# Retention, then two feed-forward layers on one core: the opening laid out by a list scheduler, the first tile in two parts, state sums of 64x64 per head

## The chip, the cores and the metric

One core of one Trainium2 chip runs the whole kernel. The metric is the device time of one execution in microseconds (us). Its engines work beside each other, each in its own order: TensorE (PE, its weight loads apart as PEld), VectorE (DVE), ScalarE (ACT), GpSimd (POOL), and SyncE (SP), which issues the DMAs. Before: 897.27 us, the median of three runs (895.79 to 897.95). About 0.3% of that, 2.7 us, is what such a measurement can tell from no change.

## The reference

```
scores = q @ k.T / sqrt(64)                  # 4 batches, 8 heads, 576 positions, 64 wide
ret    = scores * gamma_h ** (i - j)         # for i >= j, else 0;  gamma_h = 1 - 2**(-5-h)
x      = (ret @ v), heads side by side       # 2304 tokens x 512
h      = x @ w_in                            # 512 x 2048
x      = (h * cos(h)) @ w_out                # 2048 x 512
xn     = x / sqrt(mean(x*x) + 1e-6) * rms_g
out    = (silu(xn @ w_gate) * (xn @ w_val)) @ w_out2     # hidden width 1536
```

## The kernel before

**Attention.** Each batch has 576 positions: four full chunks of 128 and a rest of 64, twenty chunks in all. Chunk n costs PE four groups of float32 matmuls. `scores(n)` (L256) multiplies keys by queries, two heads at a time in the two row halves of the array; DVE then masks the result (L259). `values(n)` adds the chunk's k'v to a running sum in PSUM, the `total` (L272, one 128x128 product per pair of heads, of which only the two 64x64 blocks on the diagonal are used); ACT copies these into `state` (L282). Then `state` times the queries (L277, not in the first chunk of a batch) and the masked scores times the values (L287, in the two column halves) are summed in one bank, and DVE multiplies that with the decay and writes it to `xall` (L290). POOL scales the values first (L251). The rest chunk has no L272.

**First layer.** Tokens go in five tiles, `TILES`, four of 512 and one of 256; `ORDER_A` is 0, 1, 2, 4, 3. A tile takes 16 units, one for each 128 columns of the hidden width. A unit has `hidden` (12 matmuls: 4 slices of the contraction, each as three float32r products of high and low parts, L192 to L194), then `gate` (h cos h, three steps on ACT and three on DVE in turn, down to a high part `ghi` and a low part `glo`), and three units later (`LAG`) `out_t`, again 12 matmuls, into four accumulators `acc`. Tiles of x are split into high and low parts by `split_x` (ACT L186, DVE L129).

**Weights.** The 16 blocks of `w1` come as 64-bit floats and are turned into two float32r parts by `Block.convert`: ACT L137, DVE L141 and L142, ACT L146, DVE L147 and L148, ACT L164, DVE L129. A tile of 512 tokens can't get past a block that isn't converted. From the second tile on, the 36 pieces of the second layer's weights are converted beside the units (`piece_steps`; the units in which a piece begins stand in `begins`) and stored to DRAM, and `norm` prepares tiles 0 and 1.

**Order.** `PLAN` is the order of the loads on SP: chunk numbers, and -1 for a block of weights. The first batch's five chunks come ahead of the first unit (loop at L311), then each of the next eight units takes two chunks (`ATT_STEPS`, L731 to L763). Up to L784, the compiler's own scheduler orders all engines; after that ACT, DVE and POOL are kept in the written order (`manual_schedule(engines=ENGINES)`) and PE is still ordered by the compiler until the second layer. The chunk tiles and blocks share 14 slots (`wa`); the matmuls of attention and `hidden` share three PSUM banks (`g`) until attention ends.

**Second layer.** It runs three groups of tokens (L1012), PE in the written order, and is not touched.

Of the kernel before, what the change touches and what calls it, by code (L numbers as in the profile page):

```python
# [22 lines left out]
F32 = mybir.dt.float32  # L23
# [42 lines left out]
ATT_STEPS = 8  # L66
CONV_LEAD = 2
WARM = 10
AHEAD = 4
LAG = 3  # L70
LAST_BEGINS = [48, 51, 54, 65, 66, 67]
MANUAL = NF1

PLAN = [0, 1, 2, 3, -1, 4, 5, -1, 6, 7, -1, 8, -1, 9, 10, -1, -1, 11, 12, -1, 13, 14, -1, -1, 15, 16, -1, 17, 18, -1, 19]
# [6 lines left out]
def body(ctx: ExitStack, tc, qkv, qkr, vr, w1, w2, rg, gq, gk, mask, out):  # L81
# [57 lines left out]
    def value2(t):  # L139
        size = t.bitcast(F32)  # L140
        nc.vector.tensor_scalar(size, size, LEAST, LARGEST, op0=ALU.max, op1=ALU.min)  # L141
        nc.vector.tensor_scalar(t, t, 3, 0x3FFFFFF8, op0=ALU.logical_shift_left, op1=ALU.bitwise_and)  # L142

    def value3(t, words):
        low, high = words[..., 0], words[..., 1]
        nc.scalar.activation(low, low.bitcast(U32), AF.Copy, scale=2.0 ** -29)  # L146
        nc.vector.scalar_tensor_tensor(t, high, -2 ** 30, t, op0=ALU.bitwise_and, op1=ALU.bitwise_or)  # L147
        nc.vector.tensor_tensor(t, t, low, op=ALU.add)  # L148

    class Block:  # L150
# [7 lines left out]
        def convert(self, t):  # L158
            value1(t, self.raw)
            value2(t)  # L160
            value3(t, self.raw)
            self.w = self.where.tile([P, 2, 2, 512], F32R, tag="w", name="w")
            z = t.bitcast(F32)
            nc.scalar.copy(self.w[:, :, 0], z)  # L164
            minus(nc.vector, self.w[:, :, 1], self.w[:, :, 0], z)
# [13 lines left out]

    def split_x(t, kcs=range(KC)):  # L180
        t0, n = TILES[t]
        for kc in kcs:
            hi = xsp.tile([P, 512], F32R, tag="xs", name="xhi")
            lo = hi[:, n:] if 2 * n <= 512 else xsp.tile([P, 512], F32R, tag="xs", name="xlo")
            src = xall[:, kc, t0:t0 + n]
            nc.scalar.copy(hi[:, :n], src)  # L186
            minus(nc.vector, lo[:, :n], hi[:, :n], src)
            xs[t, kc] = (hi, lo)
# [25 lines left out]
    gam = [gam0]  # L214
# [4 lines left out]
    state = ap1.tile([P, NPAIR, P], F32, name="state")  # L219
    nc.vector.memset(state, 0.0)  # L220
    nc.vector.memset(half_pi, HALF_PI)
# [4 lines left out]
    def load(n):  # L226
# [14 lines left out]
        if 0 < n < NCH:  # L241
            gam.append(ap1.tile([P, NPAIR, width(c)], F32, name=f"gam{c}"))
            for p in range(NPAIR):
                nc.scalar.activation(gam[c][:, p, :], gam0[:, p, :width(c)], AF.Copy, scale=later[:, c, p:p + 1])

    def scores(n):
        b, c = chunks[n]
        w = width(c)
        kt, qt, vv, _ = ld[n]
        v3 = vv[:w].rearrange("p (h d) -> p h d", h=H)  # L250
        nc.gpsimd.tensor_tensor(v3, v3, vg_sb[:w, c, :].unsqueeze(2).to_broadcast([w, H, D]), op=ALU.mult)  # L251
        ps = [ps_tile().rearrange("p (h i) -> p h i", h=NPAIR) for _ in range(2)]
# [4 lines left out]
        for hh in range(2):  # L257
            s = ap.tile([P, NPAIR, P], F32, tag=f"s{hh}", bufs=2, name=f"s{hh}")
            nc.vector.tensor_tensor(s[:w, :, :w], ps[hh][:w, :, :w],  # L259
                                    mask_sb[:w, :w].unsqueeze(1).to_broadcast([w, NPAIR, w]), op=ALU.mult)  # L260
            sc[n, hh] = s

    def values(n):
        b, c = chunks[n]
        w = width(c)
        _, qt, vv, kk = ld.pop(n)
        if c < NFULL:
            if c == 0:
                total[0] = psa.tile([P, NPAIR, P], F32, tag="st", name="total")
            for p in range(NPAIR):  # L270
                cs = slice(p * P, (p + 1) * P)
                nc.tensor.matmul(total[0][:, p, :], kk[:, cs], vv[:, cs], start=c == 0 and p == 0, stop=True,  # L272
                                 skip_group_check=True)
        po = ps_tile().rearrange("p (a i) -> p a i", a=NPAIR)
        if c > 0:
            for p in range(NPAIR):
                nc.tensor.matmul(po[:, p, :w], state[:, p, :], qt[:, p, :], start=p == 0, stop=False,  # L277
                                 skip_group_check=True)
        if c < NFULL:
            for hh in range(2):  # L280
                r = slice(hh * D, (hh + 1) * D)
                nc.scalar.copy(state[r, :, r], total[0][r, :, r])  # L282
# [6 lines left out]
        t0 = b * S + c * P  # L289
        nc.vector.tensor_tensor(xall[:, :, t0:t0 + w], po[:, :, :w], gam[c], op=ALU.mult)  # L290
        del sc[n, 0], sc[n, 1]

# [5 lines left out]
    plan = list(PLAN)  # L298

    def fetch_chunks(until):  # L300

        while plan and until not in ld:
            n = plan.pop(0)
            if n < 0:
                blocks1.append(Block(w1[len(blocks1)], wa))
            else:
                load(n)

    fetch_chunks(1)
    scores(0)  # L310
    for n in range(PRO):  # L311
        fetch_chunks(n + AHEAD)
        scores(n + 1)
        values(n)
        if n == 3:
            split_x(ORDER_A[0])
            blocks1[0].convert(temps())
    blocks1[1].convert(temps())
    nc.sync.dma_start(rg_sb, rg)
    nc.scalar.mul(rg_sb, rg_sb, 0.375)  # L320

# [100 lines left out]
    pending = []  # L422

    def gate(t, f, ps, beside, copies, between=None, apart=False):

        def step():
            next(beside)
            if copies:
                copies.pop(0)()

        def finish():
            mult, cast, low = pending.pop()
            mult()
            step()
            return cast, low

        if ps is not None:
            n = TILES[t][1]
            r = ch.tile([P, 512], F32, tag="t", name="r")
            k, r = r.bitcast(I32)[:, :n], r[:, :n]  # L440
            parts = {}

            def cast():
                parts["hi"] = ch.tile([P, 512], F32R, tag="hi", bufs=LAG, name="ghi")[:, :n]
                nc.scalar.copy(parts["hi"], r)  # L445

            def low():
                parts["lo"] = ch.tile([P, 512], F32R, tag="lo", bufs=LAG, name="glo")[:, :n]
                minus(nc.vector, parts["lo"], parts["hi"], r)
                g_parts[t, f] = parts["hi"], parts["lo"]  # L450

            nc.scalar.activation(k, ps, AF.Identity, bias=quarter, scale=INV_2PI)
            old = finish() if pending else None
            nc.vector.scalar_tensor_tensor(r, k, -TWO_PI, ps, op0=ALU.mult, op1=ALU.add)  # L454
            step()
            if old:
                old[0]()
                step()
            nc.scalar.activation(r, r, AF.Sin, bias=half_pi, scale=1.0)  # L459
            step()  # L460
            if old:
                old[1]()
                step()
            pending.append((lambda: nc.vector.tensor_tensor(r, ps, r, op=ALU.mult), cast, low))  # L464
            if between:
                between()
        if pending and (ps is None or not apart):
            cast, low = finish()
            cast()
            step()  # L470
            low()
            step()
        for _ in beside:
            pass
        while copies:
            copies.pop(0)()
# [12 lines left out]
    def piece_first(k):  # L489
# [5 lines left out]
        def low():  # L495
            words = loaded[k]
            nc.scalar.activation(words[..., 0], words[..., 0].bitcast(U32), AF.Copy, scale=2.0 ** -29)

        return [size, low]

    def piece_steps(k):
# [4 lines left out]
        value2(t)  # L506
# [6 lines left out]
        nc.vector.scalar_tensor_tensor(t, words[..., 1], -2 ** 30, t, op0=ALU.bitwise_and, op1=ALU.bitwise_or)  # L513
        yield
        nc.vector.tensor_tensor(t, t, words[..., 0], op=ALU.add)
# [8 lines left out]
    begins = [i for i in range(NF1, 3 * NF1) if (i + 1) % NF1]  # L524
    begins += LAST_BEGINS

    def begun(i):
        return begins.index(i) if i in begins else None
# [169 lines left out]
    def out_t(t, f):  # L698

        n = TILES[t][1]  # L700
        if f == 0:
            accs[t] = [acc_tile(m) for m in range(KC)]
        whi, wlo = part1("out", f)
        g = g_parts.pop((t, f))
        for m in range(KC):
            c = slice(m * P, (m + 1) * P)
            mm3(accs[t][m][:, :n], (whi[:, c], wlo[:, c]), g, f == 0, f == NF1 - 1)
        if f == NF1 - 1:
# [396 lines left out]
```

## Time and profile before

| | us |
|---|---|
| median of three runs | 897.27 |
| the profiled execution | 898.45 |
| its span in the trace | 896.7 |
| PE busy | 881.8 |
| DVE busy | 663.5 |
| ACT busy | 472.6 |

The profile shows one execution. Busy time of PE overstates its work, since matmuls are pipelined and their ends modelled: from the start of one matmul to the start of the next is the better measure, and the prediction uses it. A row of the timeline merges instructions of one kind that follow each other: start, duration, engine, line, what it writes and reads, and how many. In brackets stands how long the engine idled before it, and what ended that.

### The profile page before, as it was taken

The page shows a single profiled execution, that of the slowest core. Times are in us where ns is not written, and L with a number is a line of the kernel's source. Part 1 is how long each engine was busy: PE and PEld are TensorE (multiplying, and loading weights), DVE is VectorE, ACT ScalarE, POOL GpSimd, SP SyncE. Part 2 cuts the span into 40 slices and gives each one's busy share as a digit, 9 for nine tenths or more (in the row PEclk, how much of TensorE's full clock was granted, in tenths as well). Part 3 has the DMA queues.
Part 4 walks back from the last instruction along what each step waited for, and adds up shares of the span by engine and source line. Part 5 has one row for each costly group of instructions (what it writes and reads, how often), then busy time and mean ns, then how long its engine had stood idle before and what let it go on. Part 6 is the DMA issues. An engine that isn't in the chain of part 4 may idle for free.

```text
span 896.7 us, 14175 instructions
## 1 busy us (share of the span) xinstructions
PE 881.8 (98%) x5482; PEld 803.3 (90%) x5482; DVE 663.5 (74%) x1001; ACT 472.6 (53%) x819; POOL 94.4 (11%) x97
## 2 busy tenths in 40 slices
PE   7999999999999999999999999999999999999998
PEld 6778888888888888998888999999999999999998
DVE  3999989677789777856785789789565588443584
ACT  4666567565566665655565755544443444333341
POOL 2341100000000000000445435200000000000000
PEclk9999999999999999999999999999999999999999
DMA  8966452044534443202688689998767698777693
GB/s 320 393 249 235 159 217 90 1 141 145 143 115 147 146 149 109 72 1 83 220 263 292 233 296 316 339 320 292 258 246 249 220 298 279 261 250 256 213 300 116
DMA packets 59027, 188.98 MB, mean 211 GB/s; under 512 B 5328, under 2 KB 23376, under 8 KB 50384
## 3 DMA queue, kind: packets, MB, share of 16 engines
q1 hardware_dynamic: 58960, 188.08, 61.9%
q8 instruction: 43, 0.70, 0.3%
q14 instruction: 24, 0.20, 0.1%
HBM read 140.87 MB, written 47.19 MB: 210 GB/s over the span
## 4 chain that ended last, share of the span: by engine, by line
PE 80%; DVE 12%; DMA 3%; ACT 2%; issue 1%; SPq 1%; POOL 1%; DVEq 0%; ACTq 0%; POOLq 0%
PE h L858 14%; PE acc L858 13%; PE acc L903 13%; PE acc L193 9%; PE acc L194 9%; PE acc L192 9%; DVE w L129 3%; PE h L193 3%; PE h L194 3%; PE h L192 3%; PE h L903 2%; DMA raw<-w_dram 2%; DVE s L259 1%; DVE t L147 1%; DMA so<-w 1%
## 5 line engine op out<-in xcount | busy, mean ns | idle before, releaser
L858 PE MATMUL h<-w 128*128 128x384 f32 x720 | 139.5, 335 | 1.1 <-DVE SV L840 1.1
L858 PE MATMUL acc<-w 128*128 128x384 f32 x720 | 139.9, 335 | 0.3
L858 PEld LDWEIGHTS h<-w 128*128 128x128 f32 x720 | 125.7, 188 | 2.6 <-DVE SV L840 2.2
L858 PEld LDWEIGHTS acc<-w 128*128 128x128 f32 x720 | 125.6, 188 | 1.9 <-DVE v L846 1.9
L193 PE MATMUL acc<-glo,w 128*128 128x512 f32 (+1 forms) x320 | 118.2, 369 | 0.8 <-DVE glo L129 0.8
L192 PE MATMUL acc<-ghi,w 128*128 128x512 f32 (+1 forms) x320 | 118.3, 370 | 0.0
L194 PE MATMUL acc<-ghi,w 128*128 128x512 f32 (+1 forms) x320 | 117.9, 368 | 0.0
L577 POOL TENSOR_TENSOR z<-z 128x256 f32<-128x256 f32 x72 | 66.4, 925 | 394.3 <-DMA z<-w 332.0
L903 PE MATMUL acc<-w 128*128 128x256 f32 x846 | 104.2, 283 | 0.0
L903 PEld LDWEIGHTS acc<-w 128*128 128x128 f32 x846 | 103.1, 192 | 0.3 <-DVE w L129 0.2
L193 PEld LDWEIGHTS acc<-glo,w 128*128 128x128 f32 x320 | 60.4, 189 | 11.1 <-DVE glo L129 1.2
L192 PEld LDWEIGHTS acc<-ghi,w 128*128 128x128 f32 x320 | 60.3, 189 | 10.1
L194 PEld LDWEIGHTS acc<-ghi,w 128*128 128x128 f32 x320 | 60.3, 189 | 9.9
L846 DVE TENSOR_TENSOR v<-s,acc 128x384 f32<-128x384 f32 x54 | 29.8, 552 | 52.9 <-PE acc L858 39.0
L459 ACT ACTIVATE r<-r,half_pi 128x512 f32<-128x512 f32 (+1 forms) x80 | 54.9, 686 | 11.4 <-DVE r L454 11.1
L129 DVE TENSOR_TENSOR w<-SV,w 128x768 fp32r<-128x768 f32 x55 | 50.7, 966 | 13.5 <-ACT w L886 13.5
L886 ACT CAST w<-SV 128x768 fp32r<-128x768 f32 x55 | 42.5, 831 | 34.1 <-DVE SV L891 18.3
L824 ACT COPY s<-h 128x384 f32<-128x384 f32 x54 | 25.9, 479 | 58.2 <-PE h L858 56.8
L129 DVE TENSOR_TENSOR glo<-r,ghi 128x512 fp32r<-128x512 f32 (+1 forms) x80 | 52.5, 656 | 3.9 <-ACT ghi L445 2.9
L445 ACT CAST ghi<-r 128x512 fp32r<-128x512 f32 (+1 forms) x80 | 46.3, 578 | 15.5 <-DVE r L464 15.4
L840 DVE TENSOR_TENSOR SV<-s,h 128x384 f32<-128x384 f32 x54 | 29.8, 551 | 31.5 <-PE h L858 26.2
L192 PE MATMUL acc<-xhi,w 128*128 128x512 f32 (+1 forms) x144 | 52.7, 366 | 0.0
(129 smaller groups left out, 1660.5 us busy)
## 6 DMA issues: line engine op xcount, KB each, us to landing
w<-so SPq DMA_DIRECT2D x42, 768.0 KB, 6.2
w<-s SPq DMA_DIRECT2D x24, 1024.0 KB, 5.0
raw<-w_dram SPq DMA_DIRECT2D x36, 512.0 KB, 4.0
w<-s SPq DMA_DIRECT2D x24, 768.0 KB, 4.3
raw<-w_dram SPq DMA_DIRECT2D x16, 1024.0 KB, 6.2
x<-qkv_dram SPq DMA_DIRECT2D x15, 1024.0 KB, 10.5
s<-w SPq DMA_DIRECT2D x12, 1024.0 KB, 6.9
w<-t SPq DMA_DIRECT2D x36, 256.0 KB, 2.3
```

Of the source, the lines that this page charges most:

```text
L129: eng.tensor_tensor(dst, src, hi.bitcast(F32), op=ALU.subtract)
L192: nc.tensor.matmul(dst, a[0], b[0], start=start, stop=False)
L193: nc.tensor.matmul(dst, a[0], b[1], start=False, stop=False)
L194: nc.tensor.matmul(dst, a[1], b[0], start=False, stop=stop)
L445: nc.scalar.copy(parts["hi"], r)
L459: nc.scalar.activation(r, r, AF.Sin, bias=half_pi, scale=1.0)
L577: nc.gpsimd.tensor_tensor(z[:, dst], z[:, a], z[:, b], op=op)
L840: nc.vector.tensor_tensor(dst, s, bank, op=ALU.add)
L846: nc.vector.tensor_tensor(t, s, bank, op=ALU.add)
L858: nc.tensor.matmul(bank, w[:, wp, kc * P:(kc + 1) * P], x[:, kc], start=k in (0, 1, 3) and kc == 0 and m == 0, stop=kc == 1 and m == 2, sk ...
L886: nc.scalar.copy(t[:, 0], src)
L903: nc.tensor.matmul(bank, s[:, a, i % 2, m * P:(m + 1) * P], wi[:, b], start=start and i == 0 and p == 0 and m % 2 == 0, stop=i == NPR - 1 ...
```

## The change

The constants: the first tile is cut into units 0 to 5 and 6 to 15, with all of tile 1 between them; the list of loads and the units in which pieces of the second layer's weights begin follow from that.

```
+FIRST = 6
+SEGMENTS = [(0, 0, FIRST), (1, 0, NF1), (0, FIRST, NF1), (2, 0, NF1), (4, 0, NF1), (3, 0, NF1)]
+STEPS = [(s, t, f) for s, (t, a, b) in enumerate(SEGMENTS) for f in range(a, b)]
+ENDS = [k for k in range(len(STEPS)) if k + 1 == len(STEPS) or STEPS[k][0] != STEPS[k + 1][0]]
+MANUAL = FIRST + NF1
+BEGINS = [k for k in range(MANUAL, 3 * NF1) if k not in ENDS] + list(range(3 * NF1, 4 * NF1, 2)) + list(range(4 * NF1, 4 * NF1 + 4))
-PLAN = [0, 1, 2, 3, -1, 4, 5, -1, 6, 7, -1, 8, -1, 9, 10, -1, -1, 11, 12, -1, 13, 14, -1, -1, 15, 16, -1, 17, 18, -1, 19]
+PLAN = [0, 1, 2, 3, 4, 5, 6, 7, 8, 9, 10, -1, 11, -1, 12, 13, -1, 14, -1, 15, -1, 16, -1, 17, -1, -1, 18, -1, 19, -1, -1, -1, -1, -1, -1, -1]
```

So eight of the 36 pieces begin in the units of tile 4, where three did. The parts of x of tile 0 are stored to DRAM and read back for its second part, and that part is added to what the first left in `xall`:

```
+    def keep_x(t):
+        for kc in range(KC):
+            for part in range(2):
+                nc.sync.dma_start(kept_x[:, kc, part], xs[t, kc][part].bitcast(F32))
+    def fetch_x(t):
+        for kc in range(KC):
+            xs[t, kc] = tuple(xsp.tile([P, 512], F32R, tag="xs", name=name) for name in ("xhi", "xlo"))
+            for part in range(2):
+                nc.sync.dma_start(xs[t, kc][part].bitcast(F32), kept_x[:, kc, part])
...
-            copies = [lambda m=m: nc.scalar.copy(xall[:, m, t0:t0 + n], accs[t][m][:, :n]) for m in range(KC)]
...
+            if begin == 0:
+                copies = [lambda m=m: nc.scalar.copy(x(m), accs[s][m][:, :n]) for m in range(KC)]
             else:
-                late["moves"] = copies
-            if t in ORDER_A[:2]:
+                copies = [lambda m=m: nc.vector.tensor_tensor(x(m), x(m), accs[s][m][:, :n], op=ALU.add) for m in range(KC)]
+            late["copies" if i == LAST - 1 else "moves"] = copies
+            if t in ORDER_A[:2] and end == NF1:
                 background.extend(norm(t))
```

The sums of k'v go per head, into the two column halves, and `values` is cut into functions, with the state's product ahead of the sums:

```
+    def sums_kv(n):
...
+            total[0] = psa.tile([P, NPAIR, D], F32, tag="st", name="total")
+        for h in range(H):
+            r, cs = slice(h % 2 * D, (h % 2 + 1) * D), slice(h * D, (h + 1) * D)
+            nc.tensor.matmul(total[0][r, h // 2, :], kk[:, cs], vv[:, cs], start=c == 0 and h < 2, stop=True,
+                             skip_group_check=True)
+    def copy_state(n, hh):
+        r = slice(hh * D, (hh + 1) * D)
+        nc.scalar.copy(state[r, :, r], total[0][r])
```

The opening, now the first 22 units and all of attention, is written as tasks with an engine, a price in us, what they come after, the buffers that they take and give, and a key. `lay_out` plays them through with these prices and writes the instructions in the order that results; PE, ACT, DVE and POOL are kept in it.

```
+    begin.enter_context(tc.manual_schedule(engines=ENGINES | {mybir.EngineType.PE}))
...
+            for engine, found in best.items():
+                first = min(b for b, _ in found)
+                begin, x = min(((b, x) for b, x in found if b <= first + SLACK), key=lambda bx: bx[1].key)
+                picks.append((begin, x.key, x))
...
+    def opening():
+        lead = lambda n: 10.0 + 1.7 * n if n < 11 else 28.7 + 14.0 * (n - 11)
+        unit = lambda i: 41.4 + 14.5 * i if i < FIRST else 41.4 + 14.5 * FIRST + 8.8 * (i - FIRST)
...
+                kv_tasks[n] = Task("PE", 0.48, lambda n=n: sums_kv(n), [scaled[n], value_tasks.get(n - 1)] + before
...
+            at = unit(first_use[k]) - LEAD
+            a1 = Task("ACT", 1.06, lambda k=k: blocks1[k].size(temps()), [raws[k]], ones("cv"), key=at)
+            d1 = Task("DVE", 0.6, lambda k=k: blocks1[k].clamp(), [a1], key=at)
...
+            hiddens[i] = Task("PE", 2.72, lambda i=i: first_half(i), [ready_w[f], hiddens.get(i - 1)] + xs_of[s], ones("g"), give,
+                              key=at, more=0.25, mode="whole")
...
+            if i == 1:
+                Task("SP", 4.0, lambda: keep_x(0), [xs_of[0][-1], hiddens[1]], key=0.0)
...
+    opening()
+    nc.sync.dma_start(rg_sb, rg)
+    nc.scalar.mul(rg_sb, rg_sb, 0.375)
+    fetch_x(0)
...
+    for k in range(3):
+        piece_load(k)
+    for step in piece_first(0):
+        step()
+    begin.close()
+    order.enter_context(tc.manual_schedule(engines=ENGINES))
+    for i in range(MANUAL, LAST + LAG):
```

A unit's matmuls, `hidden` or `out_t`, are one task each. The keys are no times: among tasks of one engine that can start within 0.3 us of the earliest, the lowest key goes first. The table of the sine is loaded at the start, and after the last unit seven steps are pulled at a time, not six.

## Rows read from the trace of the kernel before

**Rows 1.** The page: busy time of the engines, and PE in 40 slices.
```profile
PE 881.8 (98%) x5482; PEld 803.3 (90%) x5482; DVE 663.5 (74%) x1001; ACT 472.6 (53%) x819; POOL 94.4 (11%) x97
...
PE   7999999999999999999999999999999999999998
```

**Rows 2.** Windows: PE, PEld, DVE, ACT, POOL busy (count), PE clock, DMA share, GB/s.
```profile
6.00:13.00 7.00, 4.06 (x38) 3.07 (x38) 1.29 (x2) 4.77 (x13) 1.75 (x2) 1.00 0.96 384
13.00:34.00 21.00, 19.14 (x225) 16.49 (x224) 16.18 (x22) 11.39 (x22) 7.58 (x7) 1.00 1.02 396
34.00:39.00 5.00, 4.52 (x14) 3.23 (x13) 4.96 (x7) 0.79 (x4) 1.52 (x1) 0.66 1.03 359
50.00:130.00 80.00, 78.51 (x704) 65.50 (x704) 77.39 (x104) 49.17 (x68) 14.14 (x9) 1.00 0.53 193
```

**Rows 3.** Timeline of PE, 12 to 31 us: chunks of attention.
```profile
12.27 1.16 PE L256 MATMUL g<-x 64*128 64x128 f32 x16 [1.36 <-DMA x<-qkv_dram]
...
17.12 1.06 PE L277 MATMUL g<-x,state 128*128 128x128 f32 x8
18.11 1.09 PE L287 MATMUL g<-s,x 128*64 128x128 f32 x16
19.13 1.16 PE L256 MATMUL g<-x 64*128 64x128 f32 x16
20.22 1.16 PE L272 MATMUL total<-x 128*128 128x128 f32 x8
21.22 1.06 PE L277 MATMUL g<-x,state 128*128 128x128 f32 x8
...
28.99 1.10 PE L277 MATMUL g<-x,state 128*128 128x64 f32 x8
30.02 0.68 PE L287 MATMUL g<-s,x 64*64 64x64 f32 x16
30.64 1.16 PE L272 MATMUL total<-x 128*128 128x128 f32 x8
```

**Rows 4.** Timeline of PE, two units of the first layer.
```profile
130.35 0.39 PE L192 MATMUL h<-xhi,w 128*128 128x512 f32 x1
...
133.07 0.39 PE L192 MATMUL acc<-ghi,w 128*128 128x512 f32 x1
```

**Rows 5.** PE groups by form, 0 to 130.3 us: count, busy, mean ns.
```profile
L192 PE MATMUL g<-xhi,w 128*128 128x512 f32 x32 | 14.0, 436 | 1.2 <-ACT w L164 0.7 <-DVE s L259 0.4
...
L192 PE MATMUL acc<-ghi,w 128*128 128x512 f32 x22 | 9.1, 414 | 0.0
```

**Rows 6.** PE's waits, 6 to 130 us: total, times, longest (first and last).
```profile
PE total L272 <- DMA x<-qkv_dram: 1.6, 1, 1.6
...
PE g L277 <- DVE s L259: 0.3, 1, 0.3
```

**Rows 7.** Timeline of PE at 36 us: two matmuls of the first unit.
```profile
36.19 0.63 PE L194 MATMUL g<-xhi,w 128*128 128x512 f32 x1
36.62 0.63 PE L192 MATMUL g<-xhi,w 128*128 128x512 f32 x1
```

**Rows 8.** DVE on tile t: busy (count), PE clock, DMA share, GB/s.
```profile
0.00:130.00 130.00, 60.36 (x59) 0.99 0.70 259
```

**Rows 9.** The same for tile r, the gates' own.
```profile
0.00:130.00 130.00, 16.52 (x23) 0.99 0.70 259
```

**Rows 10.** The same for tile s, the masked scores.
```profile
0.00:130.00 130.00, 23.78 (x40) 0.99 0.70 259
```

**Rows 11.** The same for xall (20 results of attention, 4 splits).
```profile
0.00:130.00 130.00, 16.34 (x24) 0.99 0.70 259
```

**Rows 12.** DMA issues: count, KB each, median us from issue to landing.
```profile
w<-t SPq DMA_DIRECT2D x36, 256.0 KB, 2.3
```

**Rows 13.** Window of tile 4's units, columns as in the second group.
```profile
355.00:402.00 47.00, 47.00 (x367) 45.79 (x366) 30.80 (x68) 25.56 (x57) 0.00 (x0) 1.00 0.15 43
```

**Rows 14.** DVE on tile t there: two pieces of the second layer's weights.
```profile
355.00:402.00 47.00, 4.45 (x8) 1.00 0.15 43
```

More of the change, by code (lines that the diff above doesn't have):

```diff
@@ new lines, in from_state @@
+    def from_state(n):
+        w = width(chunks[n][1])
+        qt = ld[n][1]
+        po = outputs[n] = ps_tile().rearrange("p (a i) -> p a i", a=NPAIR)
+        for p in range(NPAIR):
+            nc.tensor.matmul(po[:, p, :w], state[:, p, :], qt[:, p, :], start=p == 0, stop=False, skip_group_check=True)
+    def sums_kv(n):
+        c = chunks[n][1]
+        _, _, vv, kk = ld[n]
+        if c == 0:
+            total[0] = psa.tile([P, NPAIR, D], F32, tag="st", name="total")
[3 more added lines that the diff above has]
+                             skip_group_check=True)
@@ L263, in values @@
+    def copy_state(n, hh):
+        r = slice(hh * D, (hh + 1) * D)
+        nc.scalar.copy(state[r, :, r], total[0][r])
     def values(n):
-        b, c = chunks[n]
+        c = chunks[n][1]
         w = width(c)
[L266 to L282, printed above, removed]
+        vv = ld.pop(n)[2]
+        if c == 0:
+            outputs[n] = ps_tile().rearrange("p (a i) -> p a i", a=NPAIR)
@@ L429, in step @@
                 copies.pop(0)()
[L431 to L457, printed above, removed]
-                step()
[L459 to L472, printed above, removed]
+        now = gate_parts(t, f, ps) if ps is not None else []
+        old = pending.pop() if pending else []
+        for pair in ((now[:1], old[:1]), (now[1:2], ()), (old[1:2], ()), (now[2:3], ()), (old[2:], ())):
+            for group in pair:
+                for part in group:
+                    part()
+            if any(pair):
+                step()
+        if now:
+            pending.append(now[3:])
         for _ in beside:
@@ L696, in body, with out_t @@
     accs = {}
-    def out_t(t, f):
+    def out_t(i):
+        s, t, f = STEPS[i]
         n = TILES[t][1]
-        if f == 0:
-            accs[t] = [acc_tile(m) for m in range(KC)]
+        _, begin, end = SEGMENTS[s]
+        if f == begin:
+            accs[s] = [acc_tile(m) for m in range(KC)]
         whi, wlo = part1("out", f)
@@ new lines, in first_half, with close_attention, __init__ @@
+    def first_half(i):
+        _, t, f = STEPS[i]
+        halves_of[i] = gate_parts(t, f, hidden(t, f))
+    def close_attention():
+        att.close()
+        late["psh"] = pool("psh", 1, space=PSUM)
+        late["wb"] = mid.enter_context(tc.tile_pool(name="wb", bufs=NSLOT_B, reuse_waits="tile"))
+    class Task:
+        def __init__(self, engine, busy, run, after=(), take=(), give=(), key=0.0, more=0.1, mode=None, behind=None):
+            self.engine, self.busy, self.run, self.after = engine, busy, run, [a for a in after if a]
+            self.take, self.give, self.key, self.more, self.mode = dict(take), dict(give), key, more, mode
+            self.behind, self.end, self.done = behind, None, None
+            tasks.append(self)
@@ new lines, in body, with lay_out, start_of @@
+    tasks = []
+    def lay_out(stock, free):
+        mode = [None]
+        todo = list(tasks)
+        def start_of(x):
+            begin = max([free[x.engine]] + [a.end if a.engine == x.engine else a.done for a in x.after])
+            if x.mode and x.mode != mode[0]:
+                begin = max(begin, free[x.engine] + SWITCH)
+            for name, count in x.take.items():
+                if len(stock[name]) < count:
+                    return None
+                begin = max(begin, sorted(stock[name])[count - 1])
+            return begin
+        while todo:
+            best = {}
+            for x in todo:
+                if any(a.done is None for a in x.after) or x.behind and x.behind.done is None:
+                    continue
+                begin = start_of(x)
+                if begin is not None:
+                    best.setdefault(x.engine, []).append((begin, x))
+            picks = []
+            for engine, found in best.items():
+                first = min(b for b, _ in found)
+                begin, x = min(((b, x) for b, x in found if b <= first + SLACK), key=lambda bx: bx[1].key)
+                picks.append((begin, x.key, x))
+            if not picks:
+                raise ValueError(repr([(x.engine, x.take, {k: len(stock[k]) for k in x.take}, round(x.key)) for x in todo if all(a.done is not None for a in x.after)]))
+            begin, _, x = min(picks, key=lambda p: p[:2])
+            for name, count in x.take.items():
+                for when in sorted(stock[name])[:count]:
+                    stock[name].remove(when)
+            if x.mode:
+                mode[0] = x.mode
+            if x.engine == "SP":
+                free["SP"] = begin + 0.3
+                free["DMA"] = max(free["DMA"], begin + 2.0) + x.busy
+                x.end = x.done = free["DMA"]
+            else:
+                free[x.engine] = begin + x.busy
+                x.end = begin + x.busy
+                x.done = x.end + x.more
+            for name, count in x.give.items():
+                stock[name].extend([x.done] * count)
+            todo.remove(x)
+            x.run()
@@ L743, in body @@
             if early_out:
-                out_t(*steps[i - LAG])
+                out_t(i - LAG)
             gate(t, f, ps, piece_steps(begun(i)) if begun(i) is not None
-                 else other_steps(5) if i >= LAST - NF1 else iter(range(5)), late.pop("moves", []),
-                 (lambda: scores(more[0] + 1)) if more and more[0] + 1 < N else None, i >= NF1)
+                 else other_steps(5) if i >= LAST - NF1 else iter(range(5)), late.pop("moves", []))
         elif i >= LAST:
@@ L752, in body @@
                 nc.scalar.activation(spare, half_pi, AF.Silu)
-            for _ in range(6):
+            for _ in range(7):
                 pull()
-        if i >= LAG and not (i < LAST and early_out):
-            out_t(*steps[i - LAG])
-        if more:
-            values(more[0])
-            if more[0] + 2 < N:
-                scores(more[0] + 2)
-            if len(more) > 1:
-                values(more[1])
-            chunk += len(more)
-        if first:
-            while converted[0] < min(len(blocks1), i + CONV_LEAD + 1):
-                blocks1[converted[0]].convert(temps())
-                converted[0] += 1
-        if i < LAST - NF1 and (i // NF1 != 3 or 1 not in normal):
+        if i >= LAG and not early_out:
+            out_t(i - LAG)
+        if i < LAST - NF1 and (i // NF1 != 3 or 0 not in normal):
             idle()
@@ L773, in body @@
             ahead(i, i - (LAST - NF1 + LAG))
-        if i == MANUAL - 1:
-            early.close()
-            ntp = ctx.enter_context(tc.tile_pool(name="ntp", bufs=4, side="right", reuse_waits="tile"))
-            late["nt"] = ntp
-            late["cv"] = right("cv", 3)
-            for k in range(3):
-                piece_load(k)
-            order = ExitStack()
-            for step in piece_first(0):
-                step()
-            order.enter_context(tc.manual_schedule(engines=ENGINES))
-        if i == LAST_BEGINS[-1]:
-            assert len(begins) == npiece
+        if i == BEGINS[-1]:
+            assert len(BEGINS) == npiece
             early.close()
```

293 lines of the change are left out of this document (193 added, 100 removed).

## The prediction

> **What bounds the kernel now.** I read the page first: PE is busy 98% of the span, and only the first of its 40 slices is thin [rows 1]. So the time can move in two ways only: PE gets less to do, or it loses less in the opening. Next the windows: until 39 us PE has holes, between 34 and 39 us its granted clock is 0.66 (some of it at 1.2 and some at 2.4 GHz), and from 50 to 130 us PE is busy 78.5 and DVE 77.4 of 80 us [rows 2]. After 130 us PE is never idle until the second layer. Since busy PE is overstated, I count starts. In the steady part a unit's 12 matmuls take 133.07 - 130.35 = 2.72 us [rows 4]. Up to 130.35 us PE has issued 3 x 32 matmuls of `hidden` and 3 x 22 of `out_t` (the two lines shown stand for three each) [rows 5]: 162, or 13.5 groups, 36.7 us. The other 93.6 us are start, attention and loss.
>
> Attention by starts [rows 3]: state's product 18.11 - 17.12 = 0.99, values 1.02, scores 1.09, k'v sums 1.00: 4.10 a full chunk, 3.11 the first of a batch. The rest chunk: state's product 1.03, values 0.62, and I take 0.62 for its scores: 2.27. A batch is 3.11 + 3 x 4.10 + 2.27 = 17.7, four are 70.7. The first scores begin at 6.64 us, when the first queries and keys have come. So 93.6 - 6.64 - 70.7 = 16.3 us are lost. Of these, 3.55 go before chunk 1 lands at 12.27 us (5.63 us in which only scores and sums, 2.08, are done). Nine named waits add up to 7.0 us, 3.0 of them before 12.27 [rows 6]. At the low clock, matmuls start 0.43 apart instead of 0.23 [rows 7]; eight of them make 1.6. The rest, about 7, goes at changes between attention's groups and pieces of units, which are cut into each other.
>
> **The change part by part.**
>
> *State sums per head.* Sixteen times, four products of 128x128 (eight instructions, 1.00 us) become eight of 64x64 outputs over 128 rows (sixteen instructions, two column halves beside each other). No row has this form. Above it: values, whose stationary side has the same 128x64 shape but twice the moving columns, 1.02 us; then nothing is saved. Below: half of that would be 0.5. Nearest: the rest's values, with 64 moving columns in two column halves, sixteen instructions in 0.62 [rows 3]. I take 0.62: 0.38 less, 6.1 in all; bounds -0.3 to 8. The state's copies keep their size, and each chunk still changes three times between kinds of tiling.
>
> The Trainium skill speaks against this: "TensorE: Matmul & The Clock Gate", section LDWEIGHTS, prices a weight load at its columns divided by 1.2, in ns, whatever the rows; as an estimate 16 x 53 ns = 0.85 us, so that 2.4 us would be saved and not 6.1. The rest's values load 64 columns sixteen times in 0.62 us, 39 ns each [rows 3], so the price isn't met where two column halves alternate; that rows don't count agrees with my choice of row.
>
> *More attention ahead of the first unit.* Until 12.27 us the order now can do all of chunk 0: 2.73 of 5.63, a loss of 2.9. Then ten chunks, 32.3 us by the prices above, keep PE until 44.6. Loads at 396 GB/s [rows 2] bring a full chunk (1.05 MB) in 2.65 us, so chunk 10 is there at about 33 and block 0 at 35.4. Its conversion takes five steps of 1.02 us on DVE [rows 8] and three on ACT which I count alike: 8.2, ready at 43.6. So the first unit is ready as PE runs out of chunks, and the waits for halves of a block and the low clock after them have no place. Late next is block 1 and DVE: a block costs it 5.1 [rows 8], a gate 3 x 0.72 = 2.15 [rows 9], a chunk 23.78 / 20 + 16.34 / 24 = 1.87 [rows 10, 11]: 9.1 for a unit with a new block and a chunk, against 2 x 2.72 + 3.7 = 9.2 on PE.
>
> *First tile in two parts.* This is what relieves DVE: before, 16 blocks were due in 16 units; now six, and the other ten are due in units 12 to 21, when attention asks little and a unit costs DVE 5.1 + 2.15 = 7.3 in half of the units and 2.15 in the rest, over 16 x 5.44 = 87 us. So only the first six units are tight. What stays lost there: if units are never cut and never wait, about half of the 7 for changes and no waits, 4; if nothing improves, 16.3 - 3.55 = 12.8. I take the middle, 8.4. Then start, attention and loss are 6.64 + 2.9 + (70.7 - 6.1) + 8.4 = 82.5, and the opening gains 93.6 - 82.5 = 11.1 (bounds 6.7 to 15.5, with the sums as taken).
>
> *The store and the way back.* Eight stores of 256 KB behind unit 1 cost the queues 2.1 MB, 5.3 us at 396 GB/s, while blocks 3 and later are fetched ahead of a DVE that is behind anyway: nothing. Without that cover a block comes up to 5.3 us later. The way back is on the path: the slices of x become free as the last unit of tile 1 ends, and the next unit wants them. The first lands after 2.3 us [rows 12], seven more at 0.66 each: 7 us. Cover: the rest of the last unit 2.04, one `out_t` 2.72, three slices of the next unit 2.04, together 6.8. I take 1; bounds 0, and 8 x 2.3 - 6.8 = 11.6 if each lands after the other. Behind the reads on SP stand three loads of pieces; behind the first piece's two steps on ACT stands the gate of unit 22. Three finished gates give PE 8.2 us of `out_t` in the meantime.
>
> *Later.* Adding the second part on DVE instead of copying on ACT comes where DVE is not full: nothing. But tile 4's units get eight pieces where two fell into its 47 us: DVE goes from 30.8 [rows 13] by 6 x 2.22 [rows 14] to 44.1 of 47, and the norm of tile 0, which now ends late, adds up to three steps of 0.7. I take 1 us of PE waiting; bounds 0 and 4 (two gates late). The table load and the seventh step lie beside PE's work: nothing.
>
> *Sum.* 898.45 - 11.1 + 1 + 1 = 889.3 for an execution like the profiled one, which lies 1.2 above the median: 888.
>
> **Rivals.**
>
> *The column halves bring nothing* (a form of the change not doing what it says): the sums take 1.02 like values of the same stationary shape; 6.1 + 0.3 come back: 894.5, within the bound of no change or just below it. Against it: the rest's 0.62.
>
> *The opening packs almost fully*: 4 lost instead of 8.4, and no later cost: 888 - 4.4 - 2 = 881.6. For it: DVE has some 50 us less due in the first units. Against it: 9.1 against 9.2 leaves DVE no room there.
>
> *The transfer back stalls*: 11.6 instead of 1: 898.6, no change. Against it: the 396 GB/s of many transfers together.
>
> *Slower: PE and DVE alternate in the first six units.* A unit's 12 matmuls are one task, PE's order is fixed, and it can't slip a single matmul past a wait as it does now. Six rounds of 9.1 us on DVE are 55 us; if a third of this isn't beside PE's work, 18 us are lost where I count 4.4 in that place: 888 + 13.6 = 901.6. It turns slower at about 15 of the 55. For it: all of DVE's time is spoken for there, and POOL's scaling runs beside it. Against it: chunks lie ready from 36 us on and give PE 3.7 us for 1.87 of DVE.
>
> **How the numbers follow.** My forecast 0.58 (its own range 883 to 894), full packing 0.14, no gain from the halves 0.08, the transfer 0.08, slower 0.12. With a difference under 2.7 us counted as none: faster 0.72, same 0.16, slower 0.12. The range, 880 to 899, takes in all but the last case.
>
> **What would show it.** In the trace after: sums at 0.6 us by starts; chunk 10 done at about 45 us and the first unit there; 162 matmuls of units and all attention in some 119 us instead of 130; PE's waits in the opening under 8 us without a stretch at the low clock; no idle PE where unit 22 begins, beyond 1 us; DVE at nine tenths in tile 4. I am wrong if PE waits for DVE's conversions over 10 us between 45 and 110 us, if the sums stay at 1.0, or if PE idles for the reads.

## The result, and the profile after

887.71 us (median of six runs, 886.16 to 888.63) against 897.05 us before (six runs). The ratio is 0.9893, 95% interval 0.9878 to 0.9908: 9.6 us faster by the ratio (9.3 by the medians), where 888 had been forecast. The profiled execution took 887.71 us, its span is 885.9.

The page of the changed kernel, its lines of busy time and of PE's slices, and two kinds of DMA issues that are new (count, KB each, median us to landing):

```profile
PE 871.3 (98%) x5610; PEld 794.2 (90%) x5610; DVE 665.7 (75%) x1005; ACT 472.6 (53%) x819; POOL 88.1 (10%) x97
...
PE   7999999999999999999999999999999999999998
```

```profile
xhi<-kept_x SPq DMA_DIRECT2D x4, 256.0 KB, 4.2
xlo<-kept_x SPq DMA_DIRECT2D x4, 256.0 KB, 4.6
```

PE is as full as in [rows 1] and does less: 10.5 us less busy time, 7.9 of it in the sums. The same windows as in [rows 2], and the 47 us of tile 4, which now begin ten earlier, for [rows 13] (PE, PEld, DVE, ACT, POOL busy, PE's clock, DMA share, GB/s):

```profile
6.00:13.00 7.00, 2.82 (x42) 2.32 (x42) 1.29 (x2) 4.78 (x16) 1.79 (x2) 0.96 0.99 392
13.00:34.00 21.00, 20.65 (x302) 18.07 (x301) 13.23 (x22) 5.70 (x15) 9.22 (x10) 0.93 1.02 380
34.00:39.00 5.00, 5.00 (x80) 4.47 (x81) 3.78 (x7) 2.92 (x4) 1.26 (x2) 1.00 1.01 415
50.00:130.00 80.00, 78.59 (x661) 64.53 (x661) 78.38 (x103) 59.51 (x82) 6.60 (x6) 1.00 0.66 254
...
345.00:392.00 47.00, 47.00 (x365) 45.45 (x364) 40.15 (x87) 31.07 (x67) 0.00 (x0) 1.00 0.37 117
```

The hole at the first unit (34 to 39 us) is gone, with the low clock in it. A low clock now stands earlier, behind the holes at 6 to 13 us. From 50 to 130 us PE and DVE are both as full as before. The timeline of PE shows the start, and one chunk for [rows 3]:

```profile
6.20 1.16 PE L313 MATMUL g<-x 64*128 64x128 f32 x16
9.85 0.69 PE L335 MATMUL total<-x 128*64 128x64 f32 x16 [2.49 <-DMA x<-qkv_dram]
12.23 1.95 PE L313 MATMUL g<-x 64*128 64x128 f32 x16 [1.70 <-DMA x<-qkv_dram]
14.11 1.91 PE L353 MATMUL g<-s,x 128*64 128x128 f32 x16
15.95 1.16 PE L313 MATMUL g<-x 64*128 64x128 f32 x16
...
19.62 1.16 PE L313 MATMUL g<-x 64*128 64x128 f32 x16
20.71 1.16 PE L326 MATMUL g<-x,state 128*128 128x128 f32 x8
21.80 0.69 PE L335 MATMUL total<-x 128*64 128x64 f32 x16
22.32 1.05 PE L353 MATMUL g<-s,x 128*64 128x128 f32 x16
23.29 0.68 PE L313 MATMUL g<-x 64*64 64x64 f32 x16
...
54.35 0.50 PE L240 MATMUL g<-xhi,w 128*128 128x512 f32 x1 [1.01 <-DVE xall L360]
```

By starts: scores 1.09, state's product 1.09, sums 0.52, values 0.97, in all 3.67 a full chunk where it was 4.10. The last row is the first matmul of a unit. At 12.23 and 14.11 two groups take 1.88 and 1.84 us, at the lower of the two clock levels, after holes of 2.49 and 1.70 us. Values of chunk 0 (the row at 14.11) stand behind scores of chunk 1, so they couldn't fill the second hole.

To compare the openings I use one number, as in the prediction: the start of the next matmul of a unit at about 140 us (200 us), less 2.72 / 12 us for each such matmul started till then. That is start, attention and loss. It was 93.6 before and is 81.7 after at 140 us, 82.4 at 200 us: 11.9 and 11.2 gained, forecast 11.1. The second layer's first group begins at 479.45 instead of 490.06, and the span ends 10.8 us earlier. That is more than 9.6, since the execution profiled before lay 1.4 us above its median.

The same 11.9 us can be split by PE's rows up to 140 us. Attention's groups take 66.0 us instead of 74.8 (sums 8.6 instead of 16.9), units lose 2.2 us less beyond their 2.72 for twelve matmuls, and the start is 0.4 earlier. PE's waits hardly changed: from 6 us on they are 6.8 us instead of 7.0.

### The profile page after: what moved, and what is told of

It is laid out like the page before. It is cut to its first block, busy times and chain, and to the rows that moved or that the text cites. A ratio compares the mean times of both kernels' runs of the same rounds, so it can differ in the third digit from the quotient of the medians.

```text
span 885.9 us, 14456 instructions
## 1 busy us (share of the span) xinstructions
PE 871.3 (98%) x5610; PEld 794.2 (90%) x5610; DVE 665.7 (75%) x1005; ACT 472.6 (53%) x819; POOL 88.1 (10%) x97
## 4 chain that ended last, share of the span: by engine, by line
PE 81%; DVE 7%; DMA 5%; issue 2%; ACT 2%; SPq 1%; POOL 1%; DVEq 0%; ACTq 0%; POOLq 0%
PE acc L1083 13%; PE h L1038 13%; PE acc L1038 13%; PE acc L240 8%; PE acc L241 8%; PE acc L242 8%; DMA raw<-w_dram 3%; PE h L240 3%; PE h L242 3%; PE h L241 3%; DVE w L134 2%; PE h L1083 2%; PE g L313 2%; PE g L353 2%; PE g L326 1%
## 5 line engine op out<-in xcount | busy, mean ns | idle before, releaser
L240 PEld LDWEIGHTS acc<-ghi,w 128*128 128x128 f32 x320 | 60.4, 189 | 11.1 <-ACT xall L748 0.6
L241 PEld LDWEIGHTS acc<-glo,w 128*128 128x128 f32 x320 | 60.3, 189 | 10.9 <-DVE glo L134 1.2
L480 ACT ACTIVATE r<-r,half_pi 128x512 f32<-128x512 f32 (+1 forms) x80 | 54.8, 685 | 10.5 <-DVE r L477 10.0
L240 PE MATMUL h<-xhi,w 128*128 128x512 f32 (+1 forms) x144 | 52.7, 366 | 0.0
```

What stands on the lines that cost most here:

```text
L240: nc.tensor.matmul(dst, a[0], b[0], start=start, stop=False)
L241: nc.tensor.matmul(dst, a[0], b[1], start=False, stop=False)
L480: nc.scalar.activation(s["r"], s["r"], AF.Sin, bias=half_pi, scale=1.0)
```

## The experiments

Each ran beside the kernel before on the same chip, in five rounds; not all on one chip, so ratios compare two of them more safely than times. The ratio is to that kernel, with its 95% interval; the last two columns are the number just explained (worked out from each trace).

```
                          us       ratio   interval           at 140   at 200
before                    897.05                               93.6     93.6
changed kernel            887.71   0.9893  0.9878 to 0.9908    81.7     82.4
sums alone                902.2    1.0049  1.0031 to 1.0067   100.6    100.6
old sums                  893.38   0.9955  0.9943 to 0.9968    85.8     87.1
old sums, same order      892.78   0.9953  0.9939 to 0.9967    86.3     87.4
one part                  894.16   0.9963  0.9951 to 0.9975    83.5     90.1
planner alone             896.62   0.9988  0.9978 to 0.9999    88.0     91.8
five chunks ahead         896.3    0.9989  0.9977 to 1.0001    86.0     89.1
values of chunk 0 first   888.83   0.9907  0.9891 to 0.9923    84.0     85.2
holes filled              886.06   0.9876  0.9863 to 0.9888    80.1     81.0
holes filled, prices      892.8    0.9958  0.9945 to 0.9971    87.1     87.8
no limit                  894.04   0.9977  0.9960 to 0.9993    87.4     88.6
no limit, same order      885.4    0.9873  0.9860 to 0.9886    79.8     81.1
slack 0.25                887.52   0.9895  0.9882 to 0.9908    80.7     82.1
```

**Sums alone, in the kernel before.** Two lines of its `values`:

```
-            for p in range(NPAIR): ... matmul(total[0][:, p, :], kk[:, cs], vv[:, cs], ...)
+            for h in range(H): ... matmul(total[0][r, h // 2, :], kk[:, cs], vv[:, cs], ...)
-                nc.scalar.copy(state[r, :, r], total[0][r, :, r])
+                nc.scalar.copy(state[r, :, r], total[0][r])
```

> The kernel before with nothing but the state sums per head (64x64, two column halves); order, loads and tiles stay. Theory, that PE's work is on the path in the opening: 16 sums of 0.51 instead of 1.00 us save 7 to 8 us, so 889 to 891, about two thirds of what the whole change brought. Rival, that DVE holds PE back between 50 and 130 us there (77 of 80 us busy): PE's saving becomes waiting, 894 to 897.

902.2 us (896.99 to 905.84): both theories missed, it got slower. Part of the miss is that PE's work shrinks less than reckoned. One chunk:

```profile
18.87 1.16 PE L256 MATMUL g<-x 64*128 64x128 f32 x16
19.96 0.69 PE L272 MATMUL total<-x 128*64 128x64 f32 x16
20.57 1.16 PE L277 MATMUL g<-x,state 128*128 128x128 f32 x8
21.66 1.09 PE L287 MATMUL g<-s,x 128*64 128x128 f32 x16
22.69 0.68 PE L256 MATMUL g<-x 64*64 64x64 f32 x16
```

In this order the state's product, in another tiling, lies between sums and values. By starts the sums take 0.61, the state's product 1.09, a full chunk 3.82. Over all chunks about 4.9 us are saved, not 7 to 8. The 3.67 of the changed kernel also needs its order, with the state's product ahead of the sums. Windows of the opening, columns as above:

```profile
31.00:48.00 17.00, 15.73 (x92) 11.95 (x94) 13.89 (x17) 9.84 (x15) 5.15 (x4) 0.60 1.02 387
48.00:68.00 20.00, 17.81 (x189) 14.03 (x185) 19.55 (x25) 13.78 (x19) 4.97 (x4) 1.00 0.58 215
68.00:100.00 32.00, 31.88 (x282) 25.83 (x281) 26.37 (x36) 16.26 (x24) 2.64 (x2) 0.84 0.47 165
```

A busy PE here is a slow one: clock 0.60 over 17 us and 0.84 over 32 us. Matmuls of a unit start 0.43 us apart in the first stretch. What the clock took is about (1 - 0.60) x 17 + (1 - 0.84) x 32 = 12 us, against 1.7 by the same count in [rows 2]. PE's waits from 6 to 140 us are 10.2 us instead of 7.0. So shorter sums made holes, and in this order low clock came with them. Over its twelve executions the time goes with the mean clock (896.99 us at 0.998, 905.67 at 0.985), and even the first is hardly faster than the kernel before in the same rounds, 897.44. That the holes caused the low clock is likely from the experiment that fills holes (below), but was not tried in this kernel.

**Old sums in the changed kernel**, first planned anew at their price (0.9 us), then in the changed kernel's order:

```
-        for h in range(H): ... total[0][r, h // 2, :]
+        for p in range(NPAIR): ... total[0][:, p, :]
-                kv_tasks[n] = Task("PE", 0.48, ..., mode="columns")     # first run only
+                kv_tasks[n] = Task("PE", 0.9, ..., mode="whole")
```

> The changed kernel with the old sums (128x128 per pair of heads), priced at 0.9 us in the planner and counted as whole-array work; all else stays. Theory: 16 x 0.5 us come back to the path, 894 to 896. Rival, that the packing of the opening is what counts and the sums fill holes: 887 to 890.

> The changed kernel in its own order with the old sums (128x128 per pair of heads, 1.0 instead of 0.5 us). Theory, that the sums are on PE's path: 16 x 0.45 = 7 us, 894 to 896. Rival, that holes beside DVE take up half of it: 890 to 892.

893.38 and 892.78 us. In the same order the sums are worth 892.78 - 887.71 = 5.1 us (5.4 by the ratios), between the theory and its rival. Up to 140 us the groups themselves got longer by 7.3 us in all, and PE's waits shorter by 3.2 (3.6 instead of 6.8), so holes took up a third or a little more.

**The first tile in one part.**

```
-SEGMENTS = [(0, 0, FIRST), (1, 0, NF1), (0, FIRST, NF1), (2, 0, NF1), (4, 0, NF1), (3, 0, NF1)]
+SEGMENTS = [(0, 0, NF1), (1, 0, NF1), (2, 0, NF1), (4, 0, NF1), (3, 0, NF1)]
-MANUAL = FIRST + NF1
+MANUAL = NF1
-    fetch_x(0)          # keep_x(0) and the copies after unit 5 go too
```

> The changed kernel with the first tile in one part of 16 units: sums per head, planner and chunks ahead stay, the store and the way back of x are gone, the opening ends after 16 units, pieces of the second layer begin where they did before the change. Theory, that two parts relieve DVE: all 16 blocks are due by unit 15 again, PE waits for conversions, 892 to 897. Rival, that the order alone does it: 886.5 to 888.5.

894.16 us, as the theory said. Up to 140 us it lies 1.8 us behind the changed kernel, from 140 to 200 us another 5.9. Some of PE's waits there (timeline):

```profile
148.19 0.50 PE L242 MATMUL acc<-xhi,w 128*128 128x512 f32 x1 [0.30 <-DVE w L134]
...
153.65 0.50 PE L240 MATMUL h<-xhi,w 128*128 128x512 f32 x1 [0.18 <-ACT w L189]
...
154.97 0.50 PE L242 MATMUL h<-xhi,w 128*128 128x512 f32 x1 [0.58 <-DVE w L134]
...
161.68 0.50 PE L242 MATMUL acc<-xhi,w 128*128 128x512 f32 x1 [0.53 <-DVE w L134]
...
168.40 0.50 PE L242 MATMUL h<-xhi,w 128*128 128x512 f32 x1 [0.53 <-DVE w L134]
```

Attention is over, and every unit waits for its block: at most 0.2 us for the first half, which ACT writes, and 0.3 to 0.6 for the second, which DVE writes. With the slower starts around each wait, units follow each other at 6.7 us instead of 5.44. This is what two parts remove: in the changed kernel no wait of PE shows from 140 to 210 us.

**The planner alone**: both edits at once.

> The changed kernel with the old sums and the first tile in one part: of the change, the planner and the order of the loads are left. Theory, that the three parts add up once the planner is there (sums 5.7, two parts 6.4): 898 to 901, no better than before. Rival, that the parts overlap and one of them already frees most: 893 to 896.

896.62 us, by its interval hardly faster than before, and between the two expectations. Of the gain of 9.6 us, about 1 is the planner's alone (0.1 to 2.0 by the interval). The last columns show what became of the rest: 5.6 us are won by 140 us, and 1.8 of them are left at 200, with waits for second halves of blocks in between (0.53 us each). By the ratios, to this kernel the new sums add 2.2 us (one part), the two parts 3.0 (old sums), and both 8.5; each of these is known to about 1.5 us, and each has an order planned anew.

**Five chunks ahead.**

```
-PLAN = [0, 1, 2, 3, 4, 5, 6, 7, 8, 9, 10, -1, 11, -1, 12, 13, -1, 14, ...]
+PLAN = [0, 1, 2, 3, 4, -1, 5, -1, 6, 7, -1, 8, 9, -1, 10, -1, 11, 12, ...]
-        lead = lambda n: 10.0 + 1.7 * n if n < 11 else 28.7 + 14.0 * (n - 11)
+        lead = lambda n: 10.0 + 1.7 * n if n < 5 else 18.5 + 8.2 * (n - 5)
-        unit = lambda i: 41.4 + 14.5 * i if i < FIRST else ...
+        unit = lambda i: 27.0 + 16.9 * i if i < FIRST else ...
```

> The changed kernel with five chunks ahead of the first unit instead of eleven: list of loads and keys of the chunks (8.2 us apart from the sixth on) and units (first at 27.0, 16.9 apart) go with it; sums, planner, two parts stay. Theory, that chunks ahead are what fills PE while DVE converts the first blocks: waits for blocks and half blocks come back, 890 to 894. Rival, that the planner orders either list about as well: 886.5 to 889.

896.3 us, slower than expected. PE is busy 15.4 of the 21 us from 13 to 34, with the clock at 0.84 (20.65 and 0.93 in the changed kernel). Its longest wait there:

```profile
27.20 2.04 PE L326 MATMUL g<-x,state 128*128 128x128 f32 x8 [5.17 <-DVE xall L360]
```

This is no wait for a block, as the theory had it, but for a PSUM bank that DVE frees after four steps of the first block's conversion (21.79 to 26.45 us). Up to 140 us waits for blocks come to 1.5 us and those for such results of DVE to 7.5. So the first block does hold PE up here, but by way of attention's results. How much of it is the keys, which are set by hand, stays open.

**The holes at the start.** First by order (one more edge in the planner), then by filling:

```
-            score = Task(..., [loads[n], value_tasks.get(n - 2)], {"g": 2}, ...)
+            score = Task(..., [loads[n], value_tasks.get(n - 2 if n != 1 else 0)], {"g": 2}, ...)
```

```
 def scores(n): ...
+        if n == 0:
+            keep_warm(8)        # matmuls of ones into idle_bank
 def sums_kv(n): ...
+        if n == 0:
+            keep_warm(6)
```

> The changed kernel with one edge more in the planner: scores of chunk 1 come after values of chunk 0, which lay behind a wait for chunk 1's load. Theory, that what PE loses before 16 us is order and a low clock that follows from the hole: values of chunk 0 (1.0 us at full clock, 1.8 as run) fall into the hole, and if the clock stays up the next group also wins 0.8: 885 to 887. Rival, that the loss only moves (the chunks' loads or a later wait set the end): 887.5 to 888.5.

> The changed kernel with idle matmuls (ones times ones into the bank that the start uses) in its first two holes on PE: 8 after the scores and 6 after the sums of chunk 0; all else in the same order. Theory, that the low clock there (two groups of 1.85 us instead of 1.09 and 1.0) follows from the holes and that PE sets the pace: clock 1.00 from 6 to 34 us and 1.6 us won, 885.5 to 886.5. Rival, that DVE takes it back later (waits for DVE grow by as much): clock up all the same, 887 to 888.5.

The order gave 888.83 us, just past the rival's range and by its interval not to be told from the changed kernel; at 140 us its trace is 2.3 us behind. The start got better (clock 1.00 up to 34 us), but the new order brought waits for DVE and a clock of 0.89 between 34 and 50 us. The filling kept the order and gave 886.06 us, in the middle of what the theory said. Its windows, then its timeline:

```profile
6.00:13.00 7.00, 7.00 (x72) 5.37 (x72) 1.59 (x3) 4.80 (x17) 2.09 (x2) 1.00 0.94 380
13.00:34.00 21.00, 20.38 (x326) 18.08 (x322) 14.53 (x24) 6.19 (x17) 8.34 (x8) 1.00 1.03 377
```

```profile
7.26 2.12 PE L371 MATMUL idle_bank<-warm,ones_r 128*128 128x512 f32 x8
9.31 0.69 PE L337 MATMUL total<-x 128*64 128x64 f32 x16
9.93 1.65 PE L371 MATMUL idle_bank<-warm,ones_r 128*128 128x512 f32 x6
11.51 1.16 PE L313 MATMUL g<-x 64*128 64x128 f32 x16
12.60 1.09 PE L357 MATMUL g<-s,x 128*64 128x128 f32 x16
```

With the holes filled the two groups take 1.09 us or less by starts instead of 1.88 and 1.84. At 140 us the trace is 1.6 us ahead (81.7 to 80.1), but not all of that is the clock: chunk 1 also came 0.7 us earlier here (11.51 instead of 12.23), and single traces of one order of PE differ by 1 us (below). The interval overlaps that of the changed kernel, too. The clocks of the executions speak for the cause: all four here have a mean of 1.000, the changed kernel's six 0.996 to 1.000, and its one at 1.000 is its fastest, 886.16 us. So the size, 1 to 2 us, is likely and not sharply measured.

**Less work on DVE**: the limit on the size of the first layer's weights left out, first with the task taken from the planner, then with the task kept and nothing issued.

```
-            d1 = Task("DVE", 0.6, lambda k=k: blocks1[k].clamp(), [a1], key=at)
+            d1 = Task("DVE", 0.6, lambda: None, [a1], key=at)               # second run
```

> The changed kernel without the limit on the size (one of DVE's five steps) in the conversion of the first layer's 16 blocks, which only very small and very large weights need; DVE has 0.6 us less a block, 3.6 in the six that the first part wants, 9.6 in all. Theory, that DVE sets the pace from 39 to 130 us: PE's waits there shrink, 883 to 886. Rival, that PE sets it: 887 to 888.5.

> The changed kernel in its own order, the planner's prices as they are, but the limit on the size of the first layer's weights is not issued (16 instructions of 0.6 us fewer on DVE). Theory, that the slower run without the limit was slower by the order that the planner made of the lower price: in the old order less work can only help, and since DVE is busy 78 of 80 us from 50 to 130, 2 to 5 us are won, 883 to 886. Rival, that DVE is full but doesn't set the pace: 887 to 888.5. If it is again near 894, the order was not the cause.

894.04 us planned anew, 885.4 us in the old order. The same work is left out; 8.6 us lie in the order alone. In the old order DVE is busy 10.9 us less (654.8 instead of 665.7), and 2.3 us are won (1.8 by the ratios, whose intervals overlap a little): DVE holds PE back, but by about a fifth of its time. PE is then busy 80.00 of the 80 us from 50 to 130.

**How much is an order's luck?**

```
-SLACK = 0.3
+SLACK = 0.25
```

> The changed kernel with the planner's slack at 0.25 us instead of 0.3: no work changes, a few instructions of DVE and ACT change places, PE's order stays. It measures how much of a difference between two planned orders is luck. Theory: 886 to 890, within 2 us. Rival, that a few places are worth as much as the experiments' differences: 891 or more.

887.52 us: PE's order stays and the time too. At 140 us this trace is 1.0 us ahead of the changed kernel's, half of it because chunk 1 was there earlier (11.71 instead of 12.23 us); a difference of 1 us between two traces shows nothing by itself. And with the holes filled, the planner's prices moved towards the measured starts:

```
-            score = Task("PE", 0.9 if full else 0.45, ...
+            score = Task("PE", 1.0 if full else 0.55, ...     # state 0.9 to 1.0, sums 0.48 to 0.51, values 0.83 to 0.98
```

> The changed kernel with the filled holes and the planner's prices for attention's groups on PE set to the measured starts (scores 1.0 beside a change of tiling of 0.1, state's product 1.0, sums 0.51, values 0.98). Theory, that an order planned with truer prices waits less: 883.5 to 886. Rival, that the order's luck is larger than what truer prices bring: anything from 884 to 892.

892.8 us, 6.7 more than with the old prices, past the end of the rival's range. Its timelines of PE, ACT and DVE show the worst place:

```profile
35.23 1.16 PE L313 MATMUL g<-x 64*128 64x128 f32 x16
39.51 2.04 PE L328 MATMUL g<-x,state 128*128 128x128 f32 x8 [3.11 <-DVE xall L364]
41.48 1.12 PE L337 MATMUL total<-x 128*64 128x64 f32 x16
...
36.91 1.12 ACT L142 ACTIVATE t<-raw 128x1024 f32<-128x1024 f32 x1 [6.68 <-DMA raw<-w_dram]
...
38.07 0.69 DVE L146 TENSOR_SCALAR t<-t 128x1024 f32<-128x1024 f32 x1 [3.74 <-ACT t L142]
38.68 0.68 DVE L364 TENSOR_TENSOR xall<-g,gam 128x512 f32<-128x512 f32 x1
```

PE stands 3.11 us at the head of its queue for a PSUM bank that DVE frees, and goes on at the low clock (1.97 us for what takes 1.09). DVE was idle until 38.07: it stood 3.74 us before a step of the first block, that step waited for ACT, and ACT for the block's load. The result that frees the bank comes behind the step in DVE's order. Why the truer prices lead to this order is not shown.

## Why the prediction was right, point by point

- **What bounds it.** Right: only the opening changed. Of 10.8 us of span, 11.2 were won by 200 us and about half a microsecond lost later. Of the two ways named there it was mainly the first, PE has less to do: 8.8 of the 11.9 us at 140 us are shorter groups of attention, and PE's waits stay.
- **The sums.** Taken as 0.62 us, measured 0.52 by starts; the form alone takes 0.61 (sums alone), and the rest is that values in the same tiling now follow. Attention fell from 70.7 to 4 x (2.59 + 3 x 3.67 + 2.26) = 63.4, 7.3 less instead of 6.1 (2.59 is a batch's first chunk, 2.26 its rest). The weight load's price in the Trainium skill ("TensorE: Matmul & The Clock Gate", section LDWEIGHTS), as an estimate 53 ns for 64 columns, isn't met: sixteen in 0.52 us are 32 ns each. The prediction took it that all of the saving reaches the end; in the same order about two thirds do.
- **The head.** Mis-sized: 2.9 us of loss before chunk 1 were forecast, 12.23 - 6.20 - 1.09 - 0.51 = 4.4 measured. Of the 1.5 more, 1.0 is values of chunk 0, laid behind scores of chunk 1; 0.4 is that the first scores begin earlier, at 6.20 instead of 6.64, which the sum has back in its first term. "Without a stretch at the low clock" was wrong: 1.6 us go there, as much as before, only earlier. The rest of the loss came to 81.7 - 6.2 - 63.4 - 4.4 = 7.7, with the low clock in it, where 8.4 was taken. That the forecast met the time within 0.3 us is luck in part: errors of 1.2 to 1.5 us of opposite sign, in sums and head, cancel.
- **The first unit.** Wrong in place: it begins at 54.35 us, not 44.6. The block lands at 36.4, a microsecond after what was reckoned, but its eight steps end at 48.2: masks and results of attention go between them on DVE. Chunk 10 is done at 49.6, not 45, and chunk 11 and the scores of chunk 12 go ahead of the unit. That cost little, since they gave PE its work, which was the argument against the slower rival. From 45 to 110 us PE waits 1.4 us, and none of it for a block, where over 10 would have been the sign of being wrong.
- **Two parts relieve DVE.** Right, and shown: in one part 5.9 us are lost from 140 to 200 us, to waits for blocks. That the first six units leave DVE no room (9.1 against 9.2) fits the run with less work on DVE in the same order, where PE is busy 80.00 of the 80 us from 50 to 130 instead of 78.59.
- **The store and the way back.** The store was taken as nothing: up to 140 us no wait of PE that shows is for a block. For the way back 1 us was taken; the number grows from 81.7 to 82.4 between 140 and 200 us, all of it from 194 to 196 us, where the reads are landing. The eight reads land at 4.2 to 4.6 us each, but together: PE takes single slices of x as they come, between matmuls of `out_t`.
- **Tile 4.** 1 us was taken, and PE never waits there; DVE is at 40.2 of 47, not 44 to 46; seven of the eight pieces fall into that window.
- **The rivals.** No gain from the halves: refuted. Full packing: not reached; with the holes filled, 80.1 at 140 us against its 78. The stall of the transfer back: 0.7 us instead of 11.6. The slower one didn't happen (by its own sum it would lose 2.7 us at 16.4 of the 55, not at 15), but its kind is real: three other orders of nearly the same work (limit left out, prices, five chunks) lose 6 to 9 us, and in them PE waits 5.7, 8.4 and 8.4 us for DVE up to 140 us, where it is 2.6 in the changed kernel.

## What to carry to other kernels

Parts of a change need not add up. Here shorter matmuls made the old order slower, the planner alone won about 1 us, and together with two parts they were worth 9.6. What a part wins early can be lost again at the next limit: with the tile in one part, most of what planner and sums had won by 140 us went into waits for blocks before 200. Where a program lays out the order, test a part in the same order, with its instruction left out or swapped and its price kept; planned anew, the order's luck can be larger than the part (6 to 9 us in three of these runs; under 1 in the old sums and with the other slack). An order that is fixed on every engine also passes a late load on: PE stood 3.11 us behind DVE, DVE behind ACT and ACT behind the load. Holes of a few us ahead of dense work on PE can cost twice, as waiting and as clock, and idle matmuls in them can give the second part back.

## What the runs showed of the hardware

- Sixteen float32 instructions of 128x64 weights and 64 moving columns in two column halves start within 0.52 us where values in the same tiling follow. Where a group in another tiling follows they take 0.61 (sums alone), like 64x64 weights in that place, 0.62 [rows 3]. Behind such sums values took 0.97 instead of 1.02.
- The clock went to its lower level after holes of 2.49 and 1.70 us around a short group (changed kernel), after one of 3.11 us (prices), and with holes of no more than 0.8 us between small matmuls (sums alone, 31 us on, where it stayed low for most of 17 us). It stayed at the higher level where idle matmuls filled the first two, and also in the kernel before, with holes of 1.6 and 1.4 us around the same short group [rows 2, 3, 6]. In six executions of the changed kernel the mean clock ran from 0.996 to 1.000, so the order alone doesn't settle it.
